# Per-head constants by broadcast and strided DMA in place of TensorE products, with eleven zero products first on TensorE and a redrawn order of instructions

## The chip, the cores and the metric

One core of a Trainium2 chip. The metric is the device time of one execution in microseconds; lower is better. The profile's span is some 2 us shorter than the time. Two kernels are the same when they differ by less than 2%. Medians and ratios are of fast runs alone (some executions are slower, with a lower clock on record or over 1.5% above the fastest of their kernel; they are left out). Ratios are the mean time of one kernel's fast runs over that of the kernel before in the same rounds on the same chip, so not quite the ratio of the medians beside them.

## The reference

A linear attention with decay over 4 batches, 8 heads, 768 steps, 48 columns; its output, 3072 x 384, goes through a feed-forward layer of 2048 with squared relu.

```python
for t in range(S):                       # S = 768
    cur = einsum('bhd,bhe->bhde', u[None] * kt, vt)
    y[:, :, t] = einsum('bhd,bhde->bhe', rt, state + cur)
    state = w[None, :, :, None] * state + einsum('bhd,bhe->bhde', kt, vt)
# then, with x = y as 3072 x 384:
h = maximum(x @ w_in, 0); out = (h * h) @ w_out
```

u and w have 8 x 48 numbers. The kernel needs u on all 128 partitions (`ub`), w on all of them (`wb`), and each head's w as a column over partitions (`wcol`), for the decay of the state.

## The kernel before

Work is cut into 24 units (6 chunks of 128 steps, 4 batches). A list scheduler in Python, fed with estimated costs and a table of 125 nudges (216 in the changed kernel; each shifts one operation or names its engine), fixes the order of instructions on each engine at build time. Inside an engine, nothing overtakes.

```python
    wb = const.tile([128, HD], F32)
    wrow = const.tile([1, H, PAD], F32)
    urow = const.tile([1, HD], F32)
    zb = const.tile([128, 512], BF16)
    ones = const.tile([1, 128], F32)
    nc.scalar.dma_start(out=wb, ...)      # w to 128 partitions, a broadcast (cut)
    nc.vector.memset(wrow, 1.0)
    nc.scalar.dma_start(out=urow, in_=u.rearrange("(o h) d -> o (h d)", o=1))
    nc.scalar.dma_start(out=wrow[:, :, :D], in_=w.rearrange("(o h) d -> o h d", o=1))
    # ... then w_in_sb, w_out_sb, 8 tiles each of kt, rt, vt, and all others ...

    def column_w(e):                      # w as columns: products with a vector of one
        for p in range(NP):
            nc.tensor.matmul(out=psv(wc_p, 512)[:, p : p + 1],
                lhsT=wrow[:, 2 * p : 2 * p + 2, :].rearrange("o h d -> o (h d)"),
                rhs=ones[:, :1], start=True, stop=True, skip_group_check=True)

    def spread_u(e):                      # u to 128 partitions
        nc.tensor.matmul(out=psv(ub_p, HD), lhsT=ones, rhs=urow, start=True, stop=True)
```

For the first 8 units TensorE transposes (k and r with decay); for the other 16 a transposing DMA does (`rkT<-krp`), and another one turns the result (`xt<-yb`). Zero products (`bank<-zb`) fill gaps of TensorE in the first 25 us, to keep its clock up.

## Time and profile before

| | before |
|---|---|
| time, median (range), three runs before the prediction | 178.08 us (177.42 to 178.13) |
| span | 175.7 us |
| useful TensorE work started by 30 us | 12.4 of 151.4 us |
| lost before 30 us / after it / behind the last matmul | 17.6 / 2.3 / 4.4 us |

"Useful work" is every matmul but zero products and the products for u and w, each at its usual start-to-start spacing in the trace. Counting it by start time shows where TensorE is behind, which its busy share does not: modelled busy time was 95% of the span.

The transfers of the loads (queue: packets, MB, share of 16 engines over the span; then size of each issue and median us to landing), of the kernel before:

```profile
q1 hardware_dynamic: 101888, 24.65, 67.2%
...
kt<-in_k_dram SPq DMA_DIRECT2D x24, 192.0 KB, 3.2
rt<-in_r_dram SPq DMA_DIRECT2D x24, 192.0 KB, 3.7
vt<-in_v_dram SPq DMA_DIRECT2D x24, 192.0 KB, 3.9
```

The 16 engines spend 0.672 x 175.7 = 118 us on this queue. And the waits of TensorE between 60 and 130 us (who waited for whom: us in total, times, longest):

```profile
PE bank L608 <- DMA rkT<-krp: 0.4, 1, 0.4
```

One wait of 0.4 us: the long middle is full.

### The profile page before, as it was taken

How to read it: one execution, taken by the hardware profiler on the slowest of the kernel's cores; microseconds unless marked ns; L12 is line 12 of the kernel's file. 1: busy time of each engine (PE TensorE's matmuls, PEld its weight loads, DVE VectorE, ACT ScalarE, POOL GpSimd, SP SyncE). 2: the span in 40 equal slices, each digit the busy share in tenths (PEclk: the TensorE clock that was granted, in tenths of full speed). 3: DMA queues.
4: the chain of work that ended last, by engine and by line, in shares of the span. 5: the costliest groups of instructions: out<-in, count | busy, mean ns of one | idle time of the engine just before them, and what ended most of it. 6: DMA issues, size and time to landing. Idle time of an engine off the chain costs nothing.

```text
span 175.7 us, 4385 instructions
## 1 busy us (share of the span) xinstructions
PE 167.3 (95%) x1667; PEld 120.3 (68%) x1667; DVE 131.3 (75%) x244; ACT 116.9 (67%) x234; POOL 111.2 (63%) x135
## 2 busy tenths in 40 slices
PE   5899899999999999999999999999999999999990
PEld 1554778776876777686787686777777776777860
DVE  6977898796696776895699798869875785765820
ACT  2783899984688687388476795787496562744531
POOL 3059028935999999989968967583999970000200
PEclk9999999999999999999999999999999999999998
DMA  5999999998997899798797889788979962310112
GB/s 87 211 204 179 201 185 166 145 178 159 257 229 145 197 207 212 152 186 190 152 207 174 178 190 216 151 215 187 189 155 177 189 193 49 113 27 0 48 41 94
DMA packets 106198, 28.27 MB, mean 161 GB/s; under 512 B 99009, under 2 KB 106178, under 8 KB 106178
## 3 DMA queue, kind: packets, MB, share of 16 engines
q1 hardware_dynamic: 101888, 24.65, 67.2%
q0 software_dynamic: 4128, 3.15, 12.4%
q10 hardware_dynamic: 162, 0.20, 0.8%
q8 instruction: 13, 0.21, 0.5%
q14 instruction: 7, 0.06, 0.1%
HBM read 20.65 MB, written 4.72 MB: 144 GB/s over the span
## 4 chain that ended last, share of the span: by engine, by line
PE 60%; DMA 11%; DVE 9%; POOL 9%; ACT 3%; issue 3%; SPq 2%; DVEq 0%; POOLq 0%
PE bank L728 23%; PE bank L762 23%; DMA vt<-in_v_dram 6%; PE bank L608 3%; PE bank L380 3%; POOL krp L387 3%; DMA rkT<-krp 3%; DMA kt<-in_k_dram 2%; PE bank L540 2%; SPq L456 2%; PE bank L665 2%; POOL dv L387 2%; DVE krp L387 1%; DVE gr L745 1%; DVE yb L682 1%
## 5 line engine op out<-in xcount | busy, mean ns | idle before, releaser
L762 PE MATMUL bank<-w_out_sb,g 128*128 128x384 bf16 x384 | 76.3, 326 | 0.0
L728 PE MATMUL bank<-xt,w_in_sb 128*128 128x256 bf16 (+1 forms) x600 | 74.0, 268 | 0.6 <-ACT sm L596 0.5
L753 ACT ACTIVATE g<-gr 128x512 bf16<-128x512 f32 x86 | 53.1, 629 | 19.7 <-DVE gr L745 18.5
L728 PEld LDWEIGHTS <-w_in_sb 128*128 128x128 bf16 x600 | 55.6, 98 | 12.0 <-issue 0.9
L745 DVE TENSOR_SCALAR gr<-bank 128x512 f32<-128x512 f32 x62 | 42.0, 689 | 16.6 <-PE bank L728 15.7
L762 PEld LDWEIGHTS <-g 128*128 128x128 bf16 x384 | 34.7, 98 | 17.0 <-ACT g L753 0.4
L643 DVE TENSOR_TENSOR AT<-bank,smask 128x512 bf16<-128x512 f32 x48 | 31.0, 683 | 5.3 <-PE bank L608 4.6
L387 POOL TENSOR_TENSOR dv<-vb,du 128x384 f32<-128x384 bf16 x22 | 18.5, 848 | 16.9 <-DVE du L525 16.8
L747 ACT ACTIVATE gr<-bank 128x512 f32<-128x512 f32 x34 | 20.1, 594 | 8.3 <-PE bank L728 7.0
L755 POOL TENSOR_TENSOR g<-gr 128x512 bf16<-128x512 f32 x10 | 10.4, 1043 | 23.3 <-DVE gr L745 19.3
L387 POOL TENSOR_TENSOR krp<-rt,wr 128x384 bf16<-128x384 f32 x18 | 18.0, 1002 | 2.6 <-DVE rku L387 1.6
L387 POOL TENSOR_TENSOR rk<-rt,kt 128x384 f32<-128x384 f32 x18 | 18.1, 1003 | 2.1 <-DVE rku L387 1.9
L682 DVE TENSOR_TENSOR yb<-bank,dv 128x384 bf16<-128x384 f32 x24 | 13.3, 553 | 6.7 <-PE bank L665 3.9
L392 ACT COPY osb<-bank 128x384 f32<-128x384 f32 x21 | 9.3, 478 | 13.4 <-PE bank L762 13.4
L387 POOL TENSOR_TENSOR rku<-rk,ub 128x384 f32<-128x384 f32 x16 | 16.0, 1003 | 1.3 <-DVE rk L387 1.0
L600 ACT CAST sb_all<-sm 64x192 bf16<-64x192 f32 x40 | 13.9, 348 | 3.5 <-POOL sm L387 3.0
L387 POOL TENSOR_TENSOR krp<-kt,wk 128x384 bf16<-128x384 f32 x15 | 15.1, 1005 | 1.7 <-DMA kt<-in_k_dram 1.7
L392 ACT CAST vb<-vt 128x384 bf16<-128x384 f32 x24 | 12.1, 505 | 5.0 <-DMA vt<-in_v_dram 4.9
L525 DVE TENSOR_REDUCE du<-rku 128x8 f32<-128x384 f32 x24 | 12.9, 546 | 0.9 <-POOL rku L387 0.7
L586 DVE TENSOR_TENSOR sm<-bank,sm 64x192 f32<-64x192 f32 x32 | 11.2, 352 | 2.5 <-PE bank L568 2.2
L665 PE MATMUL bank<-vb,AT 128*128 128x48 bf16 x192 | 11.3, 184 | 0.0
L380 PE MATMUL bank<-zb 128*128 128x512 bf16 x25 | 9.5, 483 | 1.7 <-DVE zb L365 1.7
(65 smaller groups left out, 141.0 us busy)
## 6 DMA issues: line engine op xcount, KB each, us to landing
kt<-in_k_dram SPq DMA_DIRECT2D x24, 192.0 KB, 3.2
rt<-in_r_dram SPq DMA_DIRECT2D x24, 192.0 KB, 3.7
vt<-in_v_dram SPq DMA_DIRECT2D x24, 192.0 KB, 3.9
out_dram<-osb SPq DMA_DIRECT2D x24, 192.0 KB, 2.3
w_in_sb<-in_moe_w_in_dram POOLq DMA_DIRECT2D x3, 384.0 KB, 8.0
w_out_sb<-in_moe_w_out_dram POOLq DMA_DIRECT2D x3, 384.0 KB, 7.5
w_in_sb<-in_moe_w_in_dram POOLq DMA_DIRECT2D x2, 192.0 KB, 5.8
w_out_sb<-in_moe_w_out_dram POOLq DMA_DIRECT2D x2, 192.0 KB, 4.1
```

What stands on the lines that cost most here:

```text
L380: nc.tensor.matmul(out=banks[7], lhsT=zb[:, :128], rhs=zb, start=True, stop=True, skip_group_check=True)
L387: return lambda e: NOW[e].tensor_tensor(dst(), a(), b_(), f)
L392: nc.scalar.copy(dst(), src())
L600: halves(lambda e, rows, i, sb=sb, sm=sm: nc.scalar.copy(SM(sb)[rows, :, i, :], SM(sm)[rows])),
L643: lambda e, T=T, i=i, x=x: nc.vector.tensor_tensor(T("AT")[:, i], psv(x, NP, C), smask[:, None, :].to_broadcast([128, NP, C]), ALU.mult),
L665: nc.tensor.matmul(out=t[:, p, i, :], lhsT=T("AT")[:, i, p, :], rhs=T("vb")[:, 2 * p + i, :], start=st is None, stop=True, skip_group_chec ...
L682: lambda e, T=T, y_p=y_p: nc.vector.tensor_tensor(T("yb"), psv(y_p, HD), T("dv").rearrange("t h d -> t (h d)"), ALU.add),
L728: nc.tensor.matmul(out=out_, lhsT=w_in_sb[:, kk, (2 * f + z) * 128 : (2 * f + z + 1) * 128], rhs=rhs, start=(kk == 0), stop=(kk == NK - 1) ...
L745: nc.vector.tensor_scalar(dst, src, 0.0, None, ALU.max)
L747: nc.scalar.activation(dst, src, AF.Relu)
L753: nc.scalar.activation(dst, src, AF.Square)
L762: nc.tensor.matmul(out=psv(o_p, dm), lhsT=G()[:, 2 * f + z, i, :], rhs=w_out_sb[:, 2 * f + z, :], start=(f == 0 and z == 0), stop=(f == NH ...
```

## The change

Its intent is to take the small fp32 products from the first microseconds of TensorE, and to warm the array there with zero products.

```diff
-    wrow = const.tile([1, H, PAD], F32)
-    urow = const.tile([1, HD], F32)
+    ub = const.tile([128, H, D], F32)
+    wcol = const.tile([128, NP], F32)
     zb = const.tile([128, 512], BF16)
-    ones = const.tile([1, 128], F32)
     nc.scalar.dma_start(out=wb, ...)
@@ (cut: zb is cleared first on DVE, wcol filled with ones; wrow and ones no longer are)
-    nc.scalar.dma_start(out=urow, ...)
-    nc.scalar.dma_start(out=wrow[:, :, :D], ...)
     nc.scalar.preload_act_table_set("natural_log_exp_and_others")
+    nc.scalar.dma_start(out=ub.rearrange("p h d -> p (h d)"),
+        in_=bass.AP(tensor=u.tensor, offset=u.offset, ap=[[0, 128], [1, HD]]))
@@ behind the masks, on POOL
+        for i in range(2):
+            nc.gpsimd.dma_start(out=wcol[i * PAD : i * PAD + D],
+                in_=w.rearrange("(p i) d -> i d p", i=2)[i])
@@
-    WARM0 = 5
+    WARM0, COLD = 11, 7.0
@@ (column_w, spread_u and the copy of u are gone; dead code, identf and hmask too)
@@ (cut: all nudges are redrawn, and several estimates of the scheduler changed)
```

So instructions change places on every engine.

## The prediction

> **What bounds the kernel now.** I read the page first (busy shares, then the row of slices), then the busy time by stretch, then the chain of work that ended last for the first 20 us, then the timeline around it.
>
> ```profile
> PE 167.3 (95%) x1667; PEld 120.3 (68%) x1667; DVE 131.3 (75%) x244; ACT 116.9 (67%) x234; POOL 111.2 (63%) x135
> ```
>
> TensorE is busy nearly always. But busy is not useful: the next view has to be set against the work. Columns: stretch, length, then busy us (and instructions) of PE, PEld, DVE, ACT, POOL, then granted clock, DMA share, GB/s.
>
> ```profile
> 0.00:10.00 10.00, 7.38 (x34) 4.07 (x35) 8.21 (x20) 5.58 (x11) 2.47 (x12) 1.00 0.82 154
> 10.00:20.00 10.00, 9.52 (x102) 5.10 (x99) 8.10 (x17) 6.42 (x20) 5.77 (x7) 1.00 1.18 194
> 20.00:30.00 10.00, 9.68 (x132) 7.73 (x130) 8.56 (x18) 9.84 (x20) 4.26 (x5) 1.00 1.02 187
> 30.00:170.00 140.00, 139.06 (x1399) 102.62 (x1398) 106.42 (x192) 94.19 (x185) 98.70 (x112) 1.00 0.79 159
> ```
>
> I took the useful TensorE work from the matmul groups and the start-to-start spacing in the trace: 384 of 128x384 at 0.163 us (62.6), 552 of 128x256 at 0.109 (60.2), 48 halves of it at 0.056 (2.7), 88 transposes at 0.056 (4.9), and 560 small ones (score, value, state products) at 0.027 to 0.043 (22.4). That is some 152.5 us of the 175.7 us span. The other 23 us: after the last matmul 4.4 us go by (171.3 to 175.7, eviction and store); summing useful matmuls by start time, 12.4 us of work is started before 30 us, so 17.6 us are lost there; from 30 us to the end of the matmuls about 1.5 us are lost. So the kernel is bound by TensorE from 30 us on, with nothing to take, and by latency before that. The change is in the part before.
>
> The chain of waits there (start us, length us, what):
>
> ```profile
> 5.93 0.56 DVE krp L387
> 6.50 0.05 issue
> 6.54 0.61 PE bank L540 x4
> 7.15 1.79 PE bank L402 x8
> 8.95 0.54 PE bank L540 x4
> ```
>
> The products to be removed (L402, the columns of w) stand on the path, between the two groups of transposes of the first unit. The timeline gives them, the product for u (L408) and two groups of zero products:
>
> ```profile
> 1.72 2.31 PE L380 MATMUL bank<-zb 128*128 128x512 bf16 x5 [1.72 <-DVE zb L365]
> 4.32 1.61 PE L408 MATMUL bank<-urow,ones 1*128 1x384 f32 x2 [0.28 <-DMA urow<-in_u_dram]
> 7.08 1.86 PE L402 MATMUL bank<-ones,wrow 1*128 1x1 f32 x8
> 14.83 1.24 PE L380 MATMUL bank<-zb 128*128 128x512 bf16 x5
> ```
>
> The first five zero products take 0.43 us from start to start, the five at 14.8 us 0.215. So the array runs at half rate until about 14 us, though the granted clock reads 1.00 throughout.
>
> **What the Trainium skill says.** "TensorE: Matmul & The Clock Gate", Part 1 (the HAM clock gate): the array starts at half rate and goes to full after some 3.4 us of sustained activity, in a free-running window, about 427 ns per 512 columns cold and 216 warm. The trace agrees in both spacings; the kernel before, with its gaps from 4 to 11 us, got there late. "DMA: Bandwidth & Descriptors", Issuing engines are not separate DMA queues: transfers from all issuers share the same 16 engines. The trace agrees: while the 128 rows of wb (1536 B each) move, up to 4.3 us, the first load of k gets little done. Same page, Rules for kernel authors: a strided last dimension becomes one descriptor per element, so wcol will be 384 of 4 bytes; no trace here shows that yet.
>
> **The change part by part.**
> 1. *Products for w leave the path.* The second transposes go from 8.88 us to just behind the multiply of r (ends 7.42 us): -1.4 us on unit 0, all of it on the path. The u product and its copy (1.61 us on PE, 0.45 us on ACT) lay beside the waits for k and w: 0 on the path.
> 2. *Warm array.* Eleven zero products at 0.43 us would run from about 1.3 to 6.0 us, with five fillers behind them in the order; the array should be warm by 5 to 8 us. Transposes of unit 0 and 1 and the first scores then take 0.22 + 0.05 per four instead of 0.43, and 0.33 per eight instead of 0.54 to 0.61. On unit 0's path: 0.2 (second transposes) + 0.25 (scores) = -0.45 us. Against it: sixteen zero products cold would be 6.9 us and could hold the first transposes (6.54 us before) by up to 1 us; that is hidden, since the second ones wait for r anyway.
> 3. *The copy of the transposes moves.* For unit 0 it is on DVE in the new order: 0.69 us (its one such copy) against 1.01 on ACT: -0.3 us.
> 4. *Broadcast of u.* wb took 1.34 us of all 16 engines (the sum of its packets' time over 16). ub is the same size, issued at about 1.3 us instead of two tiny loads. The load queue is full from 3 us: packets of the twelve first loads end 0.93 us apart (4.44, 5.44, 6.38, 7.42, 8.25, 9.13 us). So all of them come about 1.3 us later, if ub goes in front. wb itself is first and should land near 4.7 us as before. Unit 0's first multiply was held by wk (5.87 us) and by k about equally; it goes to some 6.5 us, that of r from 6.87 to about 7.8. Cost on unit 0: +0.6 to +1.0 us; unit 1's k and r, used on landing (0.32 us wait at 9.25 us), +1.3 less its slack. wcol adds some 0.2 us of engine time (a guess from 9 ns per 4-byte packet).
> 5. *Weights.* They are gated by the same loads and move by 1.3 us too, the last piece from 24.0 to some 25.3. First used: the pieces land at about 15.8, 18.0, 19.4, 21.4, 24.0 and their products start at 18.1, 19.7, 22.2, 24.6, 26.5. So there are 1.7 to 3 us of slack.
> 6. *The order.* Every nudge is redrawn. In the new order 50 zero products stand against 25, all ahead of the first real feed-forward products, which come only after the scores of unit 2, then run dense; before, 8 fillers lay between and behind them. 25 more at 0.216 us is 5.4 us, meant for gaps. Relu moves 11 instructions from DVE to ACT and squares 4 from ACT to POOL; all stay below TensorE.
>
> Sum on the early path: -1.4 - 0.45 - 0.3 + 0.8 (part 4) = -1.35 us; of this only what shortens the 17.6 us counts, and ACT is full from 20 to 30 us (9.84 of 10), which may eat a part. I take -1 from this, and -0.5 for a redrawn order whose first products run dense: 178.1 - 1.5 = **176.6 us**.
>
> **Rivals.**
> - *The loads become the wait.* Both broadcasts go ahead of k, r and v, and units 0 and 1 come 1.3 us later than the removal lets them. For it: DMA share is over 1.0 from 5 us on. Against: the engine path, not the loads, holds units 2 and 3 (k of unit 2 is in before 12 us and is used at 16.7). Then 178 to 179.5.
> - *DVE blocked in order.* Its fourth work item waits for ub, its ninth (the first state) for wcol through three ACT instructions. If wcol (issued by POOL after its masks, near 2.3 us, two of about 0.8 us each) lands after 9 us, scores and masks behind it wait: +1 to +2 us, near 179.
> - *Hidden anyway.* ACT's full stretch, and g and PSUM buffers, set when the dense part begins; the early gain becomes more fillers: 177.5 to 178.2.
> - *All of it counts,* and the new order has no ACT jam at 20 to 30 us: -3 us, 175.
>
> **Range and chances.** The best case takes 3 to 3.5 us off, not the 3.56 us that 2% is; going beyond needs much of the 17.6 us that the change does not touch. The worst needs two rivals together. So 176.6, 174.4 to 179.2; faster 0.11, same 0.82, slower 0.07.
>
> **What would show it.** Removal: second transposes of unit 0 start under 8.6 us. Warmth: 128x512 products at 0.216 us apart before 8 us. Broadcast: packets of the first loads end about 1.3 us later; last weights land near 25 us. Dense part: useful work started by 30 us rises from 12.4 to 13.5 to 14 us; the loss after 30 us stays under 3 us, the tail 4.4 us. It would be wrong if the new order left holes after 30 us, if DVE stood waiting for wcol, or if the lost time before 30 us fell by over 3 us.

## More of the kernel before

All SBUF tiles come from one pool, one behind the other in the order of their declaration.

Loads of k, r and v bring 128 steps x 8 heads x 48 numbers each: 1024 rows of 192 bytes, eight rows to a partition.

## The result, and the profile after

| | before | after |
|---|---|---|
| time, median (range), four runs each | 177.75 us (177.36 to 178.13) | 183.78 us (183.34 to 184.37) |
| ratio (95% interval) | | 1.0341 (1.0297 to 1.0386) |
| span | 175.7 us | 182.2 us |
| useful work started by 30 us | 12.4 us | 9.6 us |
| lost before 30 us / after it / tail | 17.6 / 2.3 / 4.4 us | 20.4 / 5.5 / 4.8 us |
| first feed-forward product | 18.1 us | 23.6 us |

The changed kernel is 6 us slower. Of the 6.5 us of span, 2.8 are lost before 30 us, 3.2 after it. Busy time by stretch of the changed kernel, in the columns of the prediction:

```profile
0.00:10.00 10.00, 7.44 (x37) 3.12 (x37) 6.79 (x15) 4.80 (x10) 2.51 (x11) 1.00 0.87 152
10.00:20.00 10.00, 8.62 (x90) 4.51 (x92) 8.66 (x18) 3.40 (x11) 8.41 (x10) 1.00 1.23 176
20.00:30.00 10.00, 8.19 (x108) 6.25 (x108) 6.96 (x14) 8.18 (x19) 4.27 (x5) 1.00 0.99 169
```

ACT went from 6.42 to 3.40 us in the second stretch and DVE from 8.56 to 6.96 in the third: neither became the bound. All engines wait more. For what, the timeline of the changed kernel tells:

```profile
1.19 5.52 PE L401 MATMUL bank<-zb 128*128 128x512 bf16 x16 [1.19 <-DVE wcol L315]
...
7.43 0.56 DVE L408 TENSOR_TENSOR rk<-rt,kt 128x384 f32<-128x384 f32 x1 [1.04 <-DMA rt<-in_r_dram]
...
8.51 0.40 PE L545 MATMUL bank<-identb,krp 128*128 128x128 bf16 x4 [1.14 <-DVE krp L408]
...
10.77 1.00 POOL L408 TENSOR_TENSOR rk<-rt,kt 128x384 f32<-128x384 f32 x1 [7.49 <-DMA rt<-in_r_dram]
...
13.59 3.89 POOL L480 DMA_DIRECT2D w_in_sb<-in_moe_w_in_dram  x5
```

The array was warm early: the zero products are at 0.22 us from 5 us on (sixteen in 5.52 us). The second transposes of unit 0 start at 8.51 us, not 8.88, a small part of the 1.4 us hoped for: DVE waited until 7.43 us for r of unit 0. POOL sat until 10.77 us for r of unit 1, and the weights stand behind its work in POOL's order: issued at 13.6 us, where before it was 11.4. The chain of work that ended last goes this way (start us, length us, what):

```profile
6.03 4.58 DMA rt<-in_r_dram
...
10.77 1.00 POOL rk L408
...
15.93 9.71 DMA w_in_sb<-in_moe_w_in_dram
25.68 0.83 PE bank L694 x6
```

The DMA view of the changed kernel:

```profile
q1 hardware_dynamic: 101888, 24.65, 73.9%
...
kt<-in_k_dram SPq DMA_DIRECT2D x24, 192.0 KB, 3.9
rt<-in_r_dram SPq DMA_DIRECT2D x24, 192.0 KB, 4.2
vt<-in_v_dram SPq DMA_DIRECT2D x24, 192.0 KB, 4.4
```

The same packets and bytes took 0.739 x 182.2 = 135 us of the engines, not 118. By size of packet, the 73,728 rows of 192 bytes took 17.6 ns each where they had taken 15.6, or 81.1 us of 16 engines against 72.0; in the first 20 us it was 20.3 against 15.9. That is 9 of the 17 us. Some 6 more are the 256-byte packets of the transposing DMAs, 27.0 ns against 22.4; these do not follow the addresses in the runs below (27.0 in b_dma, 25.2 in b_dma_mis, 26.6 in b_wcol_same), so they are not read. The slow rows are not what two small extra transfers do: their packets end before 7 us, and the rows are slow to the end. The waits of TensorE from 60 to 130 us in the changed kernel:

```profile
PE bank L613 <- DMA rkT<-krp: 1.4, 2, 1.0
PE bank L573 <- ACT vb L413: 0.7, 1, 0.7
PE bank L694 <- DMA xt<-yb: 0.7, 1, 0.7
PE bank L694 <- ACT osb L413: 0.6, 1, 0.6
```

The middle is no longer full. So there are three suspects: slower load packets, the two new transfers, and the redrawn order.

The built programs show a difference that the diff does not name. wcol has 16 bytes per partition and takes 32. In the kernel before, zb began at byte 21632 of each partition and the first k tile at 47744, both multiples of 64. In the changed kernel zb begins at 19616 and that k tile at 45216, both 32 past a multiple of 64, and so do all tiles of loads, weights and results. (Only the constants at the end, wk and wr among them, went the other way, onto multiples of 64.)

### The profile page after: what moved, and what is told of

It is laid out like the page before. It is cut to its first block, busy times and chain, and to the rows that moved or that the text cites. A ratio compares the mean times of both kernels' runs of the same rounds, so it can differ in the third digit from the quotient of the medians.

```text
span 182.2 us, 4406 instructions
## 1 busy us (share of the span) xinstructions
PE 168.2 (92%) x1680; PEld 119.7 (66%) x1682; DVE 134.8 (74%) x245; ACT 116.2 (64%) x234; POOL 109.6 (60%) x130
## 4 chain that ended last, share of the span: by engine, by line
PE 68%; DMA 19%; POOL 4%; SPq 3%; DVE 2%; issue 1%; ACT 1%; ACTq 0%; POOLq 0%; DVEq 0%
PE bank L694 30%; PE bank L728 29%; DMA xt<-yb 5%; DMA w_in_sb<-in_moe_w_in_dram 5%; DMA w_out_sb<-in_moe_w_out_dram 3%; SPq L461 3%; DMA rkT<-krp 3%; PE bank L613 3%; DMA rt<-in_r_dram 3%; PE bank L640 2%; PE bank L635 2%; PE bank L573 1%; DVE gr L711 1%; POOL w_in_sb L480 1%; PE bank L545 1%
## 5 line engine op out<-in xcount | busy, mean ns | idle before, releaser
L728 PE MATMUL bank<-w_out_sb,g 128*128 128x384 bf16 x384 | 74.4, 326 | 0.3 <-DMA w_out_sb<-in_moe_w_out_dram 0.3
L719 ACT ACTIVATE g<-gr 128x512 bf16<-128x512 f32 x82 | 50.3, 628 | 16.9 <-DVE gr L711 15.8
L711 DVE TENSOR_SCALAR gr<-bank 128x512 f32<-128x512 f32 x51 | 34.6, 690 | 13.2 <-PE bank L694 12.4
L713 ACT ACTIVATE gr<-bank 128x512 f32<-128x512 f32 x45 | 26.2, 592 | 8.3 <-PE bank L694 7.3
L408 POOL TENSOR_TENSOR rk<-rt,kt 128x384 f32<-128x384 f32 x20 | 20.0, 1001 | 15.0 <-DMA rt<-in_r_dram 10.0
L413 ACT CAST vb<-vt 128x384 bf16<-128x384 f32 x24 | 12.2, 509 | 15.6 <-DMA vt<-in_v_dram 15.5
L408 POOL TENSOR_TENSOR dv<-vb,du 128x384 f32<-128x384 bf16 x20 | 16.6, 831 | 8.3 <-ACT gr L713 5.1
L721 POOL TENSOR_TENSOR g<-gr 128x512 bf16<-128x512 f32 x14 | 14.9, 1062 | 7.3 <-ACT gr L713 4.5
L408 POOL TENSOR_TENSOR rku<-rk,ub 128x384 f32<-128x384 f32 x14 | 14.4, 1028 | 3.7 <-DVE rk L408 2.6
L401 PE MATMUL bank<-zb 128*128 128x512 bf16 x48 | 15.1, 428 | 1.3 <-DVE wcol L315 1.2
L413 ACT COPY osb<-bank 128x384 f32<-128x384 f32 x19 | 8.8, 479 | 11.4 <-PE bank L728 11.4
L408 POOL TENSOR_TENSOR krp<-rt,wr 128x384 bf16<-128x384 f32 x15 | 15.0, 1001 | 0.5 <-DMA kt<-in_k_dram 0.5
```

What stands on the lines that cost most here:

```text
L401: nc.tensor.matmul(out=banks[7], lhsT=zb[:, :128], rhs=zb, start=True, stop=True, skip_group_check=True)
L408: return lambda e: NOW[e].tensor_tensor(dst(), a(), b_(), f)
L413: nc.scalar.copy(dst(), src())
L711: nc.vector.tensor_scalar(dst, src, 0.0, None, ALU.max)
L713: nc.scalar.activation(dst, src, AF.Relu)
L719: nc.scalar.activation(dst, src, AF.Square)
```

## The experiments

Ratios are to the kernel before. "Loads" is the mean time of a 192-byte packet over the whole run.

| run | addresses | u, w by | order | median us | ratio (95%) | loads ns |
|---|---|---|---|---|---|---|
| changed kernel | 32 past 64 | DMA | new | 183.78 | 1.0341 (1.0297 to 1.0386) | 17.6 |
| a_align | multiples of 64 | DMA | new | 181.12 | 1.0195 (1.0138 to 1.0253) | 15.7 |
| a_same | as before | DMA | new | 180.26 | 1.0157 (1.0086 to 1.0228) | 15.8 |
| a_same_again | as before | DMA | new | 180.75 | 1.0196 (1.0133 to 1.0259) | 15.7 |
| b_misalign | 32 past 64 | products | old | 180.49 | 1.0131 (1.0070 to 1.0191) | 17.1 |
| b_dma_mis | 32 past 64 | DMA | old | 182.64 | 1.0261 (1.0218 to 1.0304) | 17.6 |
| b_dma | multiples of 64 | DMA | old | 179.50 | 1.0098 (1.0054 to 1.0142) | 15.7 |
| b_dma_same | as before | DMA | old | 179.34 | 1.0108 (1.0033 to 1.0184) | 15.7 |
| b_dma_again | as before | DMA | old | 179.60 | 1.0140 (1.0087 to 1.0192) | 15.6 |

### Placement: a_align, b_misalign

```diff
 # a_align: the changed kernel
     wcol = const.tile([128, NP], F32)
+    pad = const.tile([128, 8], F32)       # never used
 # b_misalign: the kernel before
     urow = const.tile([1, HD], F32)
+    pad = const.tile([128, 8], F32)       # never used
```

> Edit: the changed kernel with one unused tile of 32 bytes per partition behind wcol, so that every later tile starts at a multiple of 64 bytes again (in the changed kernel wcol takes 32 bytes and all later tiles start 32 bytes past one). No instruction differs. Theory PLACE (the 192-byte rows of the loads are written slower where they straddle 64-byte borders; that is why their packets take 20 to 23 ns between 6 and 16 us against 15 to 16 before): packets back to 15 to 16 ns, first feed-forward product near 21.5 us instead of 23.6, lost time after 30 us back near 2 us, 178 to 180 us in all. Rival TRAFFIC AND ORDER (ub in front of the loads, and the redrawn order): nothing changes, 183.3 to 184.3 us.

> Edit: the kernel before with one unused tile of 32 bytes per partition among the first tiles, so that every later tile starts 32 bytes past a multiple of 64, as in the changed kernel. No instruction differs. PLACE: load packets go from 15 to 20 or more ns, all loads land later, 180 to 182.5 us. TRAFFIC AND ORDER: as before, 177.4 to 178.2 us.

The pad takes the changed kernel from 183.78 to 181.12 us, and slows the kernel before from 177.75 to 180.49 us, without one instruction changed. The load queue of a_align, then of b_misalign:

```profile
q1 hardware_dynamic: 101888, 24.65, 68.8%
```

```profile
q1 hardware_dynamic: 101888, 24.65, 73.7%
```

The share goes to and fro with the pad, and the load packets with it: 15.7 and 17.1 ns. (The trace of b_misalign is of its fastest run, 178.91 us.) In a_align the first feed-forward product starts at 21.0 us, not 23.6, and the useful work started by 30 us rises from 9.6 to 11.5 us. Placement is a cause in both directions, and it acts through the load packets: the packets of the weights hardly changed with the pad (86.8 ns in the changed kernel, 85.2 in a_align for w_out; 98.8 and 102.7 for the larger ones of w_in), nor did the instructions of the engines (summed over a run the difference is under 0.2 us on ACT and on POOL in each pair of runs, and -0.5 to +1.0 us on DVE). Placement is not the whole: a_align stays 1.95% over the kernel before, and the expectation of 178 to 180 us for it missed.

### The new transfers in the old order: b_dma, b_dma_mis

Both keep the kernel before's schedule: the operations for the products stay in it with their costs and emit nothing. As in the changed kernel, zb is cleared first on DVE.

```diff
 # the kernel before
+    column_w = spread_u = lambda e: None          # places kept, nothing emitted
 ...
-        nc.scalar.activation(lnc, psv(wc_p, NP), AF.Ln)
+        nc.scalar.activation(lnc, wcol, AF.Ln)
 # ub and wcol by the DMAs of the changed kernel; b_dma with the pad of a_align, b_dma_mis without
```

> Edit: the kernel before with its order of instructions kept, the products for u and w and the copy of u left out (their places in the schedule stay empty), ub and wcol by the DMAs of the changed kernel, and a pad of 32 bytes so that tiles stay at multiples of 64. TRAFFIC: ub in front of the loads puts all of them 1.3 us later: 178.5 to 179.5 us. PLACE: the DMAs as such cost little, and the path is 1.4 us shorter at the second transposes: 176.8 to 178.3 us.

> Edit: as b_dma without the pad, so that tiles lie as in the changed kernel. PLACE: 2.5 to 4.5 us slower than b_dma. TRAFFIC AND ORDER: the same as b_dma within 0.5 us. If both this and b_dma are below 179, the redrawn order has to be the cause.

b_dma_mis is 3.1 us slower than b_dma, within what placement was to cost, so this makes three pairs: 2.7, 2.7 and 3.1 us. But b_dma itself is 1% slower than before and not 0 to 0.6% faster. The theory of placement alone falls; the transfers, with the places of the products left empty, cost something at good addresses and in the old order too. The time is where TRAFFIC put it, but not for its reason: the first ten loads end 0.2 to 0.4 us later than before, not 1.3.

### Exact addresses, and each transfer alone: a_same, b_dma_same, b_ub_same, b_wcol_same

Unused tiles put every tile from zb on at exactly the address of before (ub alone stays in front).

```diff
     ub = const.tile([128, H, D], F32)
+    pad0 = const.tile([128, 128], F32)
     wcol = const.tile([128, NP], F32)
+    pad1 = const.tile([128, 376], F32)
     zb = const.tile([128, 512], BF16)
+    pad2 = const.tile([128, 128], F32)
 # a_same also: pad3 of 768 bytes behind smask, where identf and hmask were (cut)
 # b_ub_same: only u by DMA, ub in the place of urow; b_wcol_same: only w, wcol and a pad in the place of wrow
```

> Edit: the changed kernel with unused tiles of 512, 1504, 512 and 768 bytes so that every tile from zb on stands at exactly the address it has in the kernel before. The earlier pad restored multiples of 64 alone (181.1 us). If only the 64-byte remainder matters: 180.5 to 181.7 us again. If the remainder to 128 matters too (the pad left the loads at 64 past a multiple of 128): 179 to 180 us, load packets at 15 to 16 ns instead of 16 to 18.

> Edit: the kernel before in its own order, ub and wcol by DMA, and every tile at exactly the address of before. b_dma, at multiples of 64, was 179.5 us. If the remainder to 128 was the rest: 177.5 to 178.5 us, and the waits for the transposing DMA between 78 and 112 us (3.4 us in b_dma) shrink to the 1 us of before. If the two DMAs themselves cost it: 179 to 180 us.

> Edit: the kernel before in its own order and at its own addresses, u alone by broadcast DMA, its product and copy left out, the products for w kept. TRAFFIC: 1.3 us of packets ahead of the loads: 178.5 to 179.5 us. If placement and order are all: 177.4 to 178.2 us.

> Edit: the kernel before in its own order and at its own addresses, the columns of w alone by the two strided DMAs from POOL, their products left out, u kept as a product. If removing them from between the transposes of the first unit counts: 176.5 to 177.5 us. If the start is held elsewhere: 177.4 to 178.2 us.

a_same and b_dma_same are what a_align and b_dma were, so of the address only the remainder to 64 showed. b_ub_same came to 177.71 us, ratio 1.0053 (0.9971 to 1.0135), and b_wcol_same to 178.65 us, ratio 1.0090 (1.0031 to 1.0148). The first cannot be told from nothing. The second is against its expectation: without the products for w the start did get better, 13.2 us of useful work by 30 us (before 12.4), 42.8 by 60 us (before 41.7), and then it fell behind, 80.4 by 100 us (before 81.1). The loss is in waits of TensorE near 78, 91 and 110 us, most of them for the transposing DMA. That it ended slower rests on little, though: the control below reads 1.0048 for no edit at all.

### Start-up by itself: b_colafter, b_late, b_dma_same_w11, a_same_nofill

```diff
 # b_colafter: the kernel before, products for w emitted behind unit 0's second transposes,
 #             their use on ACT behind the copy of these transposes
 # b_late: the kernel before
     nc.vector.memset(sb_all, 0.0)
+    nc.vector.memset(sb_all, 0.0)
 # b_dma_same_w11: b_dma_same
-    WARM0 = 5
+    WARM0 = 11
 # a_same_nofill: a_same
-    WARM_UNTIL, WARM_FILL = 22.0, 0.85
+    WARM_UNTIL, WARM_FILL = 22.0, 0.0
```

> Edit: the kernel before, with the products for w moved behind the second transposes of the first unit, and their use on ACT behind the copy of these transposes. No DMA and no address changes. It tests step 1 of the prediction alone (1.4 us on the path of unit 0). If what is gained on unit 0 reaches the end: 176.0 to 177.0 us where before has 177.0 to 178.0. If it is used up further on, as it was with wcol by DMA (0.75 us more useful work by 30 us, yet 1.6 us slower): 177.5 to 179 us, with a wait of over 1 us for the transposing DMA near 91 us.

> Edit: the kernel before with the clearing of the state tile on DVE doubled (1.34 us more ahead of its first multiply), so the start of everything on DVE is 1 to 1.2 us later and nothing else changes. If the early part passes to the end one to one: +1.0 to +1.3 us. If part of it is slack: +0 to +0.5. If the order behind is fragile to any shift (waits for the transposing DMA near 91 and 110 us): +1.8 us or more.

> Edit: the kernel before in its own order and at its own addresses, ub and wcol by DMA (179.3 us), with eleven zero products first in place of five. The array should be at 0.22 us per product of 512 columns from about 6 us on. If a warm array helps the first units (step 2): 0.3 to 0.8 us faster than 179.3. If the first units wait for loads and for DVE and ACT anyway: the same within 0.3 us.

> Edit: the changed kernel at the addresses of before (180.3 us), with the eleven zero products but none of the 39 fillers behind them; no other instruction moves. If the fillers hold useful products up: 0.3 to 1 us faster, first feed-forward product before 21 us. If they only fill gaps: the same within 0.3 us. If the array cools down without them: slower, with transposes at 0.43 us per four.

- b_colafter: 176.19 us, ratio 0.9963 (0.9875 to 1.0051), inconclusive. The second transposes of unit 0 start at 7.48 us in it, 1.4 us earlier as predicted. By the interval, taking the products from between the transposes, with no new transfer, gains at most 1.3%.
- b_late: 178.78 us, ratio 1.0085 (1.0011 to 1.0160), 1.5 us for 1.7 us of delay (the first multiply on DVE starts at 7.65 us, not 5.93; 1 to 1.2 us had been meant). This agrees with a delay that passes to the end one to one, but the interval, 0.2 to 2.8 us, does not show it.
- b_dma_same_w11: 178.43 us (two fast runs), ratio 1.0068 (0.9963 to 1.0172), against 1.0108 and 1.0140 without: nothing that the intervals allow to read. Six more zero products warm the array by 5 us, then the first wait lets it cool (granted clock 0.76 from 10 to 20 us).
- a_same_nofill: 182.69 us, ratio 1.0303 (1.0228 to 1.0377), 2.4 us slower than a_same (by the ratios 1.0 to 1.4% over a_same_again and a_same). The 39 fillers are needed.

Why the last, two lines each from the view by stretch tell, first a_same, then a_same_nofill (after the busy times: granted clock, DMA share, GB/s):

```profile
10.00:20.00 10.00, 9.12 (x99) 5.01 (x100) 9.22 (x19) 4.95 (x17) 8.75 (x11) 1.00 1.13 189
20.00:30.00 10.00, 9.24 (x128) 7.71 (x127) 8.05 (x16) 8.58 (x17) 5.82 (x8) 1.00 1.04 183
```

```profile
10.00:20.00 10.00, 6.64 (x75) 4.85 (x75) 9.12 (x19) 4.89 (x17) 8.75 (x11) 0.50 1.16 192
20.00:30.00 10.00, 8.48 (x88) 7.06 (x87) 5.81 (x12) 6.52 (x13) 3.58 (x5) 0.66 1.07 194
```

In the second stretch the other engines do the same work in both; on TensorE the fillers are missing and the clock is halved, and it is still at 0.66 on average when the feed-forward products come, where it costs. This agrees with the Trainium skill, "TensorE: Matmul & The Clock Gate", Part 1: the array falls back to half rate behind an idle window.

### Which part is the chip: before_again, b_wcol_again, b_dma_again, a_same_again

Unedited copies of the kernel before, b_wcol_same, b_dma_same and a_same, in five rounds on one chip.

> The kernel before, unchanged, profiled again beside the others: a control. If its trace has the wait of 0.7 to 1.5 us for the transposing DMA near 91 us as well, this wait is not made by the two DMAs. If it has none, as in the first trace, it goes with any shift of the start. Time: 0.997 to 1.003 of before; this shows also how far two equal kernels differ here.

> b_wcol_same again (w alone by DMA, order and addresses of before), in five rounds: it was 1.009 of before, though more useful work was started by 30 us. If this stands: 1.005 to 1.013 again, with the wait near 91 us. If it was the chip: 0.996 to 1.003.

> b_dma_same again (both by DMA, order and addresses of before), in five rounds: it was 1.011 of before. If the two DMAs as such cost 1.5 to 2 us: 1.008 to 1.013 again. If part was the chip: 1.000 to 1.006.

> a_same again (the changed kernel at the addresses of before), in five rounds, for what the redrawn order costs over b_dma_again on the same chip: it was 0.5% over it. 0.3 to 1% again if the order costs it; 0 within 0.2% if not.

before_again took 178.10 us (1.0048, 1.0000 to 1.0096), outside the 0.997 to 1.003 expected of an unedited copy; b_wcol_again 178.57 us (1.0081, 1.0008 to 1.0154), so no more than 0.3% over that copy; the other two stand in the table. The product of scores near 92 us in before_again, then in b_wcol_again:

```profile
92.38 0.40 PE L609 MATMUL bank<-rkT 48*128 48x128 bf16 x8
```

```profile
92.94 0.40 PE L607 MATMUL bank<-rkT 48*128 48x128 bf16 x8 [0.94 <-DMA rkT<-krp]
```

The kernel before has no wait there on this chip either, though its transposed tile comes barely in time. The pair of transposing DMAs was issued at 86.75 us in before_again, at 87.45 us in b_wcol_again and at 88.73 us in b_dma_again:

```profile
86.75 3.95 SPq L551 DMA_TRANSPOSE rkT<-krp  x2
```

```profile
87.45 4.03 SPq L549 DMA_TRANSPOSE rkT<-krp  x2
```

```profile
88.73 4.12 SPq L545 DMA_TRANSPOSE rkT<-krp  x2
```

So the wait is no accident of one trace. Every variant in the old order has it, from 0.7 us (b_misalign) to 1.5 us (b_wcol_same) beyond the usual spacing of the starts, those that started later and those that started earlier; in b_late the view puts it down to ACT. A late issue is not its only source. In b_wcol_same the pair was issued at 86.11 us, earlier than in the kernel before, and was longer under way, as its chain shows:

```profile
86.11 6.67 DMA rkT<-krp
...
92.82 0.40 PE bank L607 x8
```

The kernel before needed its tile 5.4 us after the issue (86.81 to 92.19 us), without a wait. Since TensorE has no slack here, whatever comes late on SP's queue is lost.

**What stays open.** Why a kernel that is ahead at 60 us gets these transposes later, once by a later issue (b_wcol_again) and once by a longer transfer (b_wcol_same), was not isolated. The nudges were drawn for the kernel before, and SP's queue runs in order; that any shift spoils their fit is the likely reading, argued and not shown. No run beat the kernel before by more than the noise.

## Why the prediction was wrong

It said 176.6 us (174.4 to 179.2); 183.8 us was measured, 3.4% slower, where it gave slower by over 2% a chance of 0.07.

- **The step that failed is the sum: "Sum on the early path: -1.4 - 0.45 - 0.3 + 0.8 (part 4) = -1.35 us".** The time lost before 30 us did not fall by it but rose by 2.8 us, 17.6 to 20.4. The sum has no term for where the tiles lie. The change moved the tiles of the loads to 32 bytes past a multiple of 64; load packets took 17.6 ns in place of 15.6 and 2.7 to 3.1 us came of it, in three pairs of runs. The declarations in the diff and the built program had it; the part "The change part by part" asked for instructions and transfers and never for addresses.
- **"-0.5 for a redrawn order whose first products run dense" had the wrong sign.** At equal addresses the new order is 0.5 to 1.0% slower than the old one with the same transfers (a_same over b_dma_same, a_align over b_dma, a_same_again over b_dma_again), some 1 to 1.7 us. Only a_align over b_dma is clear of the noise by itself; the three agree in sign. The first products do run dense, but first at 21 to 22 us. Where the loss lies is not settled: in a_same and a_same_again useful work by 30 us is about that of the old order, and waits near 34, 88 and 97 us follow; a_align is already 1.3 us behind b_dma at 30 us and waits no more than it later.
- **Step 1 (the products leave the path, -1.4 us)** described the place rightly and the worth wrongly. The second transposes moved by 0.4 us in the changed kernel (8.51 us; "under 8.6 us" held), and by 1.3 us in b_wcol_same (7.57 us); what held them in the changed kernel is the load of r. Step 3 held as well: the copy took 0.69 us on DVE. With w alone by DMA the gain by 60 us was 0.8 to 1.1 us, and it was given back in the waits for transposes: 1.0081 and 1.0090 at the end, where an unedited copy read 1.0048. That it ended slower is not shown; that nothing of the gain was left is.
- **Step 2 (warm array)** held in its mechanism, 0.22 us spacing before 8 us, but not as a gain of its own. Its other half was missed: the fillers are worth some 2.4 us, since without them the clock falls back. ("8 fillers lay between and behind them" was a miscount: the built kernel before has 5.)
- **Step 4 (broadcast of u, loads 1.3 us later)** was too large. Its cost was read from one trace: the packets of wb took 1.34 us of 16 engines there, but 0.68 in before_again, and wb and ub together took 1.48 in the changed kernel. Nor did the first load of k get "little done" beside wb: 812 of its 1024 packets had ended by 4.3 us. At good addresses (a_same, b_dma_again) the first ten loads end 0.2 to 0.6 us later than before; u alone cost an unreadable 0.5%. In the changed kernel they end 0.2 to 1.5 us later. Part 5, the weights, was too small in turn: the packets of the last piece for the first layer end at 27.2 us, not near 25 (24.1 before), the slack of 1.7 us was used up, and TensorE waited 0.5 us for weights at 25.7. Placement made more than half of it: in a_same they are issued at 12.4 us, not 13.6, and end at 24.8.
- **"From 30 us on, with nothing to take"** was right, and the wrong conclusion was drawn from it. Nothing to take is also no slack to give: the loss there more than doubled, 2.3 to 5.5 us, where the prediction wanted it under 3.
- **The rivals.** That the loads become the wait was the right one, by slower packets and not by ub in front of them, and it was sized at 178 to 179.5. DVE blocked behind wcol did not happen: ACT read wcol at 9.50 us without a wait.

The 3.4% put together: placement 1.3 to 1.8%, the two transfers in the old order 1.0 to 1.4%, the redrawn order with its zero products 0.5 to 1.0%. The first is shown by experiments that change nothing else; how the other two shares arise is open, and each may be off by the 0.5% that an unedited copy showed.

## What to carry to other kernels

Before predicting a change that declares or removes a tile, compare the addresses of all tiles behind it in the two built programs: a tile of 16 bytes cost this kernel 1.5%, and an unused pad of 32 bytes took it back. In a kernel whose bound engine has no slack for 140 us, test an early change also by what it does to the in-order queues later; useful work counted by start time shows at once whether an early gain is kept. Keep zero products that hold the clock, and price them by taking them out.

## What the Trainium skill lacked or had wrong

- "SBUF — State Buffer", Operand start alignment, says that DMAs into SBUF are correct at element-aligned addresses; that the start address of the SBUF side has a price is on no page I found (the next point has the nearest). Here rows of 192 bytes took 17.1 to 17.6 ns per packet at 32 past a multiple of 64, against 15.6 to 15.8 at multiples of 64, and the kernels were 2.7 to 3.1 us of 178 slower.
- "DMA: Bandwidth & Descriptors", How a descriptor splits into AXI transactions, does not say whether its cuts at 256-byte borders hold on the SBUF side. If they do, rows that start at 0, 64, 128 and 192 make 1 + 1 + 2 + 2 = 6 transactions, rows at 32, 96, 160 and 224 make 1 + 2 + 2 + 2 = 7. This is an estimate from that page: 17% more; in the page's beats of 32 bytes it is 36 and 40, 11% more, also an estimate. The packets took 13% longer (17.6 over 15.6). It would fit; no run here tells it from another reason.
- The same page, Rules for kernel authors, has one descriptor per element for a strided last dimension. The prediction read this as 384 packets of 4 bytes; the trace of the changed kernel records 32 packets of 48 bytes for wcol, twelve elements each, and the two issues took 1.35 us on POOL. This does not prove the page wrong, since it lets a packet hold several descriptors elsewhere; what it lacks at this rule is what a trace will show.
- "TensorE: Matmul & The Clock Gate", Part 1, warns of its clock events. To add: in the trace of before the granted clock reads 1.00 in the first 5 us, while zero products stand 0.43 us apart, the cold rate; the first clock record of that trace is at 14.1 us, where the spacing halves. In a_same_nofill it reads 0.50 once the array has cooled. In these traces the value before the first record proves nothing; the spacing of equal products does.
